# Attention, routing and two expert layers in one launch: smaller pieces of the products, the last 32 tokens gathered as 128 quarter rows, loads moved behind the first gathers

## The chip, the cores and the metric

The kernel is one program on one core of a Trainium2 chip. Its time is the device time of one execution in microseconds (us). TensorE (PE) does the matmuls, VectorE (DVE) and ScalarE (ACT) the elementwise work, GpSimd (POOL) issues the gathers and scatters by index, SyncE (SP) issues the other DMAs. TensorE's granted clock has two levels, 2.4 GHz (1.00 in the profile) and 1.2 GHz (0.50).

## The reference

Three stages follow one another; the second decides which tokens the third computes together.

```python
# 1 attention: B 4, H 8, S 576, D 64, window of 128, linear bias
scores = where(mask, scale * q @ k.T + bias, -1e9)
x = softmax(scores) @ v                     # -> 2304 tokens x 512
# 2 routing and experts: 8 experts of cap = 288 tokens each
order = argsort(-(x @ w_gate).flatten())
for idx in order:                           # best (token, expert) pair first
    if token is free and the expert has room: assign it
out[mask] = relu(x[mask] @ w1[e]) @ w2[e]   # 512 -> 1024 -> 512
# 3 gated layer, 512 -> 1536 -> 512, every token
g = x @ w_gate;  y = (g * sigmoid(g) * (x @ w_val)) @ w_out
```

The greedy assignment is computed as rounds: the expert that fills first is found, with the threshold at which it has 288 tokens; its tokens are fixed, taken out, and the next round begins.

## The kernel before, in words

**Up to about 165 us** comes attention with the gate's logits, and then the first routing round. After it the program has eight stretches of about 75 us, one for each expert of the order found (k = 0 to 7, "expert 0" to "expert 7" here). In a stretch TensorE computes, for the 288 tokens of expert k:

- the transposes of the gathered tokens (`turn`, L1122): the tokens arrive as rows, three gathers by `fetch` (L1099, POOL) of 128, 128 and 32 rows of 512 numbers into `xg`, and are turned into four banks of 128 x 288, which are evicted as two float16 halves X (high part on ACT, L1077, low part on DVE, L1084). For a column block there are three transposes: 128 rows, 128 rows, 32 rows;
- h, 8 products of 4 contraction tiles (`layer`, L1153; each tile takes 3 matmuls of 128 x 288, for high and low parts), evicted to P; then o, 4 products of 8 tiles; then gate and value, 24 products of 4 tiles, against the weights GV; all of these stand under L1153;
- the output (L1289): for each of two blocks of 128 tokens 12 tiles of 3 matmuls of 128 x 512; the last 32 tokens of an expert are collected in `PR` and computed for four experts at once. Rows are scaled on ACT (L1294) and scattered by POOL (L1298).

Expert 0 computes in float32 (L1159, L1285) while the weights of the gated layer are still being read (36 pieces of 512 KB, tile `stg`, L324) and split on DVE and ACT. The expert's own weights come in 8 pieces of 512 KB: for expert 0 straight into WE, later through `stw`, rounded on ACT (L1055) with the rest on DVE (L1059).

**Beside this runs the routing round of the next expert** (`route`), mostly on DVE. It searches the threshold digit by digit. A digit of it is a chain: all logits are compared with the candidates (L802), summed by partition into `cn` (L806), added up over the partitions by one small matmul on TensorE (`add_up`, L810, result `rp`), and turned into the digit by short DVE instructions (L813 to L861), after which the next comparison begins. When the threshold is known, L896 and L897 (TensorE) count what lies before each token, DVE works out positions (L902 to L926) and a one-hot table `oc` (L929), L934 (TensorE, 18 matmuls) makes the list of tokens from it, and L939 to L942 (DVE) write the index table `idx`, from which the three gathers start. Round k + 1 runs during expert k.

**The order of instructions is written out by a planner** (`Plan`). Every step is added with an engine, a cost, a due time, and the steps it depends on. For each engine the planner takes the ready step with the earliest due time that can start soon (`soft` steps give way to others), with its own costs, a hand-over time between engines, and `late`, an extra delay after a step's end before anybody may use it (1.6 for DMAs). The outcome is a fixed list of instructions per engine; at run time an engine runs its list in order and waits where a step isn't ready. A step of products is one item for the planner: it can't put a count's matmul between its matmuls. h is an item of 12 matmuls, o of 24, gate and value of 12, output of 12.

**Banks**: PSUM has a ring of six banks `mm`, given out in the order in which the planner starts their first user.

Of the kernel before, what the change touches and what calls it, by code (L numbers as in the profile page):

```python
# [42 lines left out]
ROUTE = ((12, 58), (-5, 30))  # L43
WA = 7
# [9 lines left out]
HOLD = range(0, 0)  # L54
# [205 lines left out]
def body(ctx, tc, a, out):  # L260
# [55 lines left out]
    def glu_weights(c, due):  # L316
# [41 lines left out]
        add("DMA", dma(2 ** 19), due, fetch, w=[("stg", c)], late=LATE)  # L358
# [17 lines left out]
    with ExitStack() as es:  # L376
# [316 lines left out]
        for c in range(24):  # L693
            glu_weights(c, 2000 + c)
        plan.run(FIT[0], need)

# [34 lines left out]
    def route(k, due0, due1):  # L731
        v, pos = {}, [0]

        def do(engine, us, fn, r=(), w=(), chain=True):
            pos[0] += 1
            add(engine, us, due0 + (due1 - due0) * min(1.0, pos[0] / (95 if k > 1 else 45)), lambda e: fn(),
                r=[*r, *consts] if pos[0] == 1 else r, w=[("route",)] * chain + [*w], soft=k > 0, port=True)
# [218 lines left out]
        if k < E - 1:  # L956
# [5 lines left out]
            for step, bits in enumerate(FINE if fine else ()):  # L962
# [8 lines left out]
                do("DVE", cost, lambda n=n: by_partition(n))  # L971
# [66 lines left out]
    def weights(k, u):  # L1038
        for c in range(8):
# [3 lines left out]
            def fetch(e, c=c, v=v):  # L1043
                if k not in regs:
                    regs[k] = nc.sync.value_load(eid[k][0:1, 0:1], min_val=0, max_val=E - 1)
                if k == 0:
                    v["f"] = WF[:, c]
                    if c > 3:
# [40 lines left out]
    def tokens(k, u):  # L1089
# [3 lines left out]
        def rows_of(c):  # L1093
            return slice(0, 128) if c < 2 else slice(0, 32)

        def fetch(e, c):
            if ("xg", k) not in T:
                T["xg", k] = wk.tile([128, 3, DM], F32, name="xg", bufs=RINGS["xg"])
# [16 lines left out]

        def turn(e, c, kd):
            if ("X", k) not in T:
                T["X", k] = wk.tile([128, 2, 4, CAP], F16, name="X", bufs=RINGS["X"])
            if ("mm", k, "x", kd) not in T:
                T["mm", k, "x", kd] = bank()  # L1120
            r = rows_of(c)
            nc.tensor.transpose(T["mm", k, "x", kd][:, c * 128:min(CAP, c * 128 + 128)],  # L1122
                                T["xg", k][r, c, kd * 128:kd * 128 + 128], ident[r, r])

        pieces = [[(c, kd) for c in range(3)] for kd in range(4)]
        if k == 0:
            pieces = [[(c, kd) for kd in range(4)] for c in range(3)]
        for n, piece in enumerate(pieces):
            add("PE", 0.083 * len(piece), u - ta + 4 + tn * n, lambda e, piece=piece: [turn(e, *x) for x in piece],
                r=[("xg", k, c) for c, _ in piece] + [("ident",)], w=[("mm", (k, "x", kd), c) for c, kd in piece], soft=k > 0)  # L1130
        for kd in range(4 if k == 0 else 0):
            def whole(e, kd=kd):
                dst = T["X", 0].rearrange("p m k c -> p (m k c)").bitcast(F32).rearrange("p (k c) -> p k c", k=4)[:, kd]
                if e == "ACT":
                    nc.scalar.activation(dst, T["mm", 0, "x", kd][:, :CAP], AF.Copy)
                else:
                    nc.vector.tensor_copy(dst, T["mm", 0, "x", kd][:, :CAP])

            add({"ACT": act(CAP, True), "DVE": dve(CAP)}, None, u - ta + 5 + tn * kd, whole,
                r=[("mm", (k, "x", kd))] + [("mm", (k, "x", kd), c) for c in range(3)],  # L1140
                w=[("X", k, kd, "hi"), ("X", k, kd, "lo")])
        for kd in range(4 if k else 0):
            split(u - ta + 5 + tn * kd, (k, "x", kd), lambda kd=kd: T["mm", k, "x", kd], ("X", k, kd),
# [268 lines left out]
```

## Time and profile before

| what | before |
|---|---|
| median of 3 runs | 850.88 us (849.67 to 853.48) |
| profiled execution | 851.98 us, of which the span is 850.2 |
| TensorE busy | 799.9 us (94%) |
| VectorE busy | 612.7 us (72%) |
| ScalarE / GpSimd busy | 344.8 us (41%) / 138.8 us (16%) |
| TensorE waits from 165 us on: count's matmul L810 | 8.1 us, 10 times |
| TensorE waits from 165 us on: transposes L1122 for gathers | 3.6 us, 4 times |

The profile is of one execution. Its span begins with the first and ends with the last instruction; 1.78 us of the execution lie outside it. Engines run in parallel, so busy shares don't add up; with TensorE at 94%, the time is TensorE's work and its waits.

### The profile page before, as it was taken

What the parts mean: (1) busy time and instruction counts of PE and PEld (TensorE: products, weight loads), DVE (VectorE), ACT (ScalarE), POOL (GpSimd) and SP (SyncE); (2) the same over time, 40 slices, a digit from 0 to 9 for tenths busy, and PEclk for the clock granted to TensorE, in tenths of its full rate; (3) what the DMA queues carried; (4) which work ended last, traced back from release to release, by engine and by line L of the source; (5) the groups of instructions that cost most, each with busy time, mean ns of one, the idle gap of its engine ahead of it and who ended that gap; (6) DMA issues with size and microseconds to landing.
All of it is one profiled execution on the core that took longest, in us unless ns stands there. A gap on an engine that the chain in (4) does not pass through costs nothing.

```text
span 850.2 us, 16631 instructions
## 1 busy us (share of the span) xinstructions
PE 799.9 (94%) x6397; PEld 587.1 (69%) x6397; DVE 612.7 (72%) x1763; ACT 344.8 (41%) x775; POOL 138.8 (16%) x195
## 2 busy tenths in 40 slices
PE   7999994499999999999999999999999999999997
PEld 5888884267765777477667865786678677757763
DVE  3788899979999898689877887888579954312320
ACT  5788883245447424312431242135212543211220
POOL 5677653100003001100110011001100210010001
PEclk9999997589999999999999999999999999999999
DMA  8889612566564003400430051024001561000000
GB/s 265 308 302 330 213 57 81 202 234 204 182 199 165 13 1 110 141 2 1 161 91 1 11 194 61 2 75 152 25 1 54 154 221 51 1 25 1 2 1 37
DMA packets 32064, 92.08 MB, mean 108 GB/s; under 512 B 3952, under 2 KB 10480, under 8 KB 31216
## 3 DMA queue, kind: packets, MB, share of 16 engines
q1 hardware_dynamic: 29008, 81.57, 28.9%
q0 software_dynamic: 2976, 9.44, 3.2%
q8 instruction: 50, 0.82, 0.4%
q14 instruction: 30, 0.25, 0.1%
HBM read 81.56 MB, written 9.44 MB: 107 GB/s over the span
## 4 chain that ended last, share of the span: by engine, by line
PE 69%; issue 11%; DVE 11%; ACT 3%; DMA 2%; POOL 2%; SPq 0%; POOLq 0%; DVEq 0%; ACTq 0%
PE mm L1153 41%; PE mm L1289 10%; PE mm L1159 4%; PE s L549 4%; PE mm L1285 2%; PE o L609 2%; PE t L569 2%; PE mm L1122 2%; DVE cmp L802 1%; DVE cn L806 1%; DMA xg<-x_dram,idx 1%; PE rp L934 1%; DVE tl L584 1%; DVE sc L557 1%; POOL xg L1099 1%
## 5 line engine op out<-in xcount | busy, mean ns | idle before, releaser
L1153 PE MATMUL mm<-O,GV 128*128 128x288 f16 x2304 | 287.5, 286 | 0.0
L1153 PEld LDWEIGHTS <-GV 128*128 128x128 f16 x2304 | 221.9, 98 | 55.4
L1153 PEld LDWEIGHTS <-WE 128*128 128x128 f16 x1344 | 129.8, 98 | 34.2 <-issue 1.0
L1289 PE MATMUL mm<-WO,P 128*128 128x512 f16 x504 | 113.5, 383 | 0.0
L1099 POOL DMA_INDIRECT xg<-x_dram,idx x24 | 25.0, 1041 | 407.9 <-issue 241.6
L1236 ACT ACTIVATE P<-z 128x288 f16<-128x288 f32 x84 | 37.0, 441 | 127.1 <-DVE z L1228 127.1
L1289 PEld LDWEIGHTS <-P 128*128 128x128 f16 x504 | 48.7, 99 | 57.2 <-issue 2.2
L1153 PE MATMUL mm<-P,WE 128*128 128x288 f16 x672 | 84.0, 286 | 0.0
L1153 PE MATMUL mm<-X,WE 128*128 128x288 f16 x672 | 83.9, 286 | 0.0
L1059 DVE SCALAR_TENSOR_TENSOR WE<-stw,WE 128x512 f16<-128x512 f32 x112 | 73.8, 685 | 12.8 <-ACT WE L1055 12.8
L1055 ACT ACTIVATE WE<-stw 128x1024 f16<-128x1024 f32 x56 | 58.3, 1052 | 24.4 <-DMA stw<-in_w_dram 24.3
L1228 DVE SCALAR_TENSOR_TENSOR z<-mm,t 128x288 f32<-128x288 f32 x84 | 38.1, 454 | 38.7 <-PE mm L1153 36.1
L806 DVE TENSOR_REDUCE cn<-cmp 128x56 f16<-128x1008 f16 (+2 forms) x55 | 63.8, 1160 | 1.0
L549 PE MATMUL s<-kt,qb 128*128 128x192 f32 (+2 forms) x288 | 58.0, 336 | 5.1 <-DMA kt<-in_kT_dram 5.1
L802 DVE TENSOR_TENSOR cmp<-wm,thr 128x1008 f16<-128x1008 f32 (+1 forms) x50 | 61.0, 1221 | 1.2
L1222 ACT ACTIVATE t<-mm 128x288 f32<-128x288 f32 x96 | 39.1, 407 | 56.0 <-PE mm L1153 54.0
L563 ACT ACTIVATE pb<-sc,mx 128x192 f32<-128x192 f32 (+2 forms) x144 | 56.2, 432 | 10.3 <-DVE mx L557 9.9
L1298 POOL DMA_INDIRECT out_dram<-R,idx x16 | 17.9, 1117 | 239.4 <-ACT R L1294 223.1
L1239 DVE TENSOR_TENSOR P<-z,P 128x288 f16<-128x288 f32 x84 | 38.3, 456 | 20.4 <-ACT P L1236 20.1
L557 DVE CUSTOM_DVE_ANT_0 sc<-s,bias 128x192 f32<-128x192 f32 (+2 forms) x144 | 41.9, 330 | 14.1 <-PE s L549 5.9
L549 PEld LDWEIGHTS s<-kt,qb 128*128 128x128 f32 x288 | 46.7, 203 | 6.8 <-DMA qb<-in_qB_dram 3.9
L1082 DVE SCALAR_TENSOR_TENSOR P<-mm,P 128x288 f16<-128x288 f32 x56 | 25.4, 453 | 28.6 <-ACT P L1077 28.5
(166 smaller groups left out, 1090.8 us busy)
## 6 DMA issues: line engine op xcount, KB each, us to landing
stw<-in_w_dram SPq DMA_DIRECT2D x56, 512.0 KB, 3.9
stg<-in_glu_dram SPq DMA_DIRECT2D x36, 512.0 KB, 4.1
qb<-in_qB_dram SPq DMA_DIRECT2D x3, 2304.0 KB, 10.9
x_dram<-xr SPq DMA_DIRECT2D x16, 256.0 KB, 3.5
WE<-in_w_dram SPq DMA_DIRECT2D x8, 512.0 KB, 5.5
kt<-in_kT_dram SPq DMA_DIRECT2D x3, 1152.0 KB, 7.4
vf<-in_vN_dram SPq DMA_DIRECT2D x8, 256.0 KB, 4.1
vt<-in_vT_dram SPq DMA_DIRECT2D x4, 512.0 KB, 7.9
```

Of the source, the lines that this page charges most:

```text
L549: nc.tensor.matmul(v["s"][:, par, c:], QB[b % 2][:, hp * 9 + i], KT[b % 2][:, hp, (i - 2) * 64 + c:(i + 1) * 64], start=True, stop=True)
L557: nc.vector.tensor_tensor_reduce(out=v["sc"][:, par, c:], in0=v["s"][:, par, c:], in1=bias[:, hp, c:], scale=-0.125, scalar=3.0e38, op0=OP ...
L563: nc.scalar.activation(PB[n % NPB][:, par, 64 * par + c:64 * par + W], v["sc"][:, par, c:], AF.Exp, bias=v["mx"][:, par:par + 1], scale=-1.0)
L802: V.tensor_tensor(v["ca"], v["wm"][:, :, None, :].to_broadcast(by), thr[:, None, :, None].to_broadcast(by), op=OP.is_ge)
L806: V.tensor_reduce(tile_of("cn", [128, E, 8], F16, bufs=1)[:, :, :n], v["ca"], op=OP.add, axis=AX.X)
L1055: nc.scalar.activation(WE[:, c, 0], v["f"], AF.Copy, scale=sc)
L1059: nc.vector.scalar_tensor_tensor(WE[:, c, 1, at], f[:, at], sc, WE[:, c, 0, at], op0=OP.mult, op1=OP.subtract)
L1153: nc.tensor.matmul(p[:, :at.stop - at.start], w(i, k), x[:, j, k, at], start=(m == 0), stop=(m == 3 * nk - 1))
L1222: nc.scalar.activation(v["t"], T["mm", k, ("gv", f, 0)][:, :CAP], AF.Silu, scale=1.0 / (SO * SG))
L1228: nc.vector.scalar_tensor_tensor(v["z"], T["mm", k, ("gv", f, 1)][:, :CAP], SPR / (SO * SG), v["t"], op0=OP.mult, op1=OP.mult)
L1239: nc.vector.tensor_sub(P()[:, 1, f], v["z"], P()[:, 0, f])
L1289: nc.tensor.matmul(T["mm", k, "y", c], x[:, i, kk, at], WO[0][:, kk, j, :], start=(kk == 0 and i == j), stop=(kk == 11 and i == 1))
```

## The change

Four things change.

**Pieces.** Every product is added to the planner in pieces of two contraction tiles (6 matmuls in float16, 2 instructions in float32), and the output too. The arithmetic and its order inside a product stay.

**Count.** `by_partition` has `late=0.6`, so the planner places the count's matmul later on TensorE than it did. The due times of the rounds for experts 2 to 7 are spread over 50 us where they were spread over 35.

**Gather.** The last 32 tokens are fetched as 128 quarter rows: row 4t + q of the view of x with 128 columns goes to partition 32q + i. `listed2` writes that index column with four small DVE instructions in place of one. One 128 x 128 transpose turns them all, where four transposes of 32 rows stood, so a token set has 9 transposes in place of 12, in five banks in place of four: four of 256 columns, one of 128 that holds the 32 last columns of all four blocks. X is evicted in five pairs of instructions.

**Loads.** Before the first gathers, only 11 of the gated layer's 36 weight pieces and 2 of expert 0's 8 pieces may be fetched; the others wait for the three gathers of expert 0 (a small POOL write to their buffer holds them) and come interleaved. Before the change 4 of the 8 could go ahead, and the 36 were held by their ring of three buffers alone.

```diff
-ROUTE = ((12, 58), (-5, 30))
+ROUTE = ((12, 58), (-5, 45))
-HOLD = range(0, 0)
+EARLY_GLU = 11
+HOLD = range(11, 14)
 ...
-        add("DMA", dma(2 ** 19), due, fetch, w=[("stg", c)], late=LATE)
+        add("DMA", dma(2 ** 19), due, fetch, r=[("xg", 0, x) for x in range(3)] if c >= EARLY_GLU else [], w=[("stg", c)], late=LATE)
 ...
             V.tensor_scalar(p2, v["pi"][:, :2], float(N // 2), None, op0=OP.add)
-            V.tensor_scalar(idx[k][:, 2:], v["pi"][:, 2:3], float(N // 2), None, op0=OP.add)
             V.tensor_sub(idx[k][:, :2], p2, v["pi"][:, 1:3])
+            for q in range(4):
+                V.tensor_scalar(idx[k][32 * q:32 * q + 32, 2:], v["pi"][:32, 2:3], 4.0, 2.0 * N + q, op0=OP.mult, op1=OP.add)
 ...
-                do("DVE", cost, lambda n=n: by_partition(n))
+                do("DVE", cost, lambda n=n: by_partition(n), late=0.6)
 ...
-                when = u - WA + (3.9 * c if c < 4 else 15.6 + 3.9 * (c - 4))
-                add("DMA", dma(2 ** 19), when, fetch, r=[("eid", k)] + [("xg", k, x) for x in range(3 if c > 3 else 0)],
+                when = u - WA + 3.9 * c if c < 4 else glu_due(EARLY_GLU + 2 * (c - 4) + 1) + 0.5
+                add("DMA", dma(2 ** 19), when, fetch, r=[("eid", k)] + [("xg", k, x) for x in range(3 if c > 1 else 0)],
 ...
-                out=T["xg", k][rows_of(c), c, :], out_offset=None, in_=x_dram[:, :],
-                in_offset=bass.IndirectOffsetOnAxis(ap=idx[k][rows_of(c), c:c + 1], axis=0))
+                out=T["xg", k][:, part(c)], out_offset=None,
+                in_=x_dram[:, :] if c < 2 else x_dram.rearrange("n (q d) -> (n q) d", q=4),
+                in_offset=bass.IndirectOffsetOnAxis(ap=idx[k][:, c:c + 1], axis=0))
 ...
-        pieces = [[(c, kd) for c in range(3)] for kd in range(4)]
+        pieces = [[(c, kd) for c in range(2)] for kd in range(4)] + [[(2, 4)]]
 ...
-            add("PE", (3 if by is layer else 4) * nk * pe(at.stop - at.start), when, fn, r=r, w=[("mm", (k, name)), ("in order",)])
+            for k0 in range(0, nk, 2):
+                def fn(e, k0=k0):
+                    if k0 == 0:
+                        T["mm", k, name] = bank()
+                    by(T["mm", k, name], w, x(), nk, range(k0, k0 + 2))
+                us = (3 if by is layer else 4) * pe(CAP)
+                add("PE", 2 * us, when + k0 * us, fn, r=r, w=[("mm", (k, name)), ("in order",)])
 ...
-                for kk in range(4 * a, 4 * a + 4):
+                for kk in range(2 * a, 2 * a + 2):
 ...
-            steps = [(a, c) for a in range(3)]
+            steps = [(a, c) for a in range(6)]
```

Three places show what the planner makes of it. Line numbers after the change are 2 to 24 higher. The first is TensorE at the tokens of expert 3, before: the first three of the four groups of transposes, between matmuls of expert 2's output.

```order
5198 L1289 MATMUL mm<-WO,P 128x512
5199 L1122 MATMUL mm<-cst,xg 128x128 x2
5200 L1122 MATMUL mm<-cst,xg 128x32
5201 L1122 MATMUL mm<-cst,xg 128x128 x2
5202 L1122 MATMUL mm<-cst,xg 128x32
5203 L1122 MATMUL mm<-cst,xg 128x128 x2
5204 L1122 MATMUL mm<-cst,xg 128x32
5205 L1289 LDWEIGHTS P
5206 L1289 MATMUL mm<-WO,P 128x512
```

The same place after: the fourth group follows 12 output matmuls later (two transposes), and the single transpose of the last 32 tokens another 12 later.

```order
5177 L1313 MATMUL mm<-WO,P 128x512
5178 L1128 MATMUL mm<-cst,xg 128x128 x6
5179 L1313 LDWEIGHTS P
5180 L1313 MATMUL mm<-WO,P 128x512
5181 L1313 LDWEIGHTS P
```

The nine rows of transposes have become a group of six, and what stands ahead of them is shorter: from L896 to the first transposes TensorE had 48 matmuls of gate and value, L934, then 24 of gate and value and 24 of the output, and now has 42, L934, 24 and 18.

The second is VectorE from the one-hot table to the index table of expert 3, before (`P` and `z` are evictions of the gated layer, `WE` the rest of expert 3's weights).

```order
1063 L929 TENSOR_TENSOR oc<-k_slot,po 128x2304
1064 L1239 TENSOR_TENSOR P<-z,P 128x288
1065 L1059 SCALAR_TENSOR_TENSOR WE<-stw,WE 128x512
1066 L1228 SCALAR_TENSOR_TENSOR z<-mm,t 128x288
1067 L1059 SCALAR_TENSOR_TENSOR WE<-stw,WE 128x512
1068 L1239 TENSOR_TENSOR P<-z,P 128x288
1069 L939 TENSOR_SCALAR p_6317<-rp 128x2
1070 L940 TENSOR_SCALAR idx_2989<-rp 128x1
1071 L941 TENSOR_TENSOR idx_2989<-p_6317,rp 128x2
1072 L942 TENSOR_SCALAR ridx_2994<-rp 32x1
```

And after.

```order
1066 L931 TENSOR_TENSOR oc<-k_slot,po 128x2304
1067 L1263 TENSOR_TENSOR P<-z,P 128x288
1068 L1252 SCALAR_TENSOR_TENSOR z<-mm,t 128x288
1069 L1062 SCALAR_TENSOR_TENSOR WE<-stw,WE 128x512
1070 L1263 TENSOR_TENSOR P<-z,P 128x288
1071 L941 TENSOR_SCALAR p_6323<-rp 128x2
1072 L942 TENSOR_TENSOR idx_2989<-p_6323,rp 128x2
1073 L944 TENSOR_SCALAR idx_2989<-rp 32x1 x4
1074 L945 TENSOR_SCALAR ridx_2994<-rp 32x1
```

One instruction of the weights' rest has moved behind the index table, the column for the last 32 tokens comes after that of the first 256, and it takes four instructions.

The third is SyncE's list of loads around expert 0's weights (WE) and the gated layer's (stg), before.

```order
76 L1052 DMA WE<-in_w_dram 128x1024
77 L1052 ISA
78 L1052 DMA WE<-in_w_dram 128x1024
79 L1052 ISA
80 L1052 DMA WE<-in_w_dram 128x1024
81 L324 DMA stg<-in_glu_dram 128x1024 x2
82 L1052 ISA
83 L1052 DMA WE<-in_w_dram 128x1024
```

And after.

```order
76 L1055 DMA WE<-in_w_dram 128x1024
77 L325 DMA stg<-in_glu_dram 128x1024 x2
78 L1055 ISA
79 L1055 DMA WE<-in_w_dram 128x1024
80 L1055 ISA
81 L1055 DMA WE<-in_w_dram 128x1024
82 L325 DMA stg<-in_glu_dram 128x1024 x2
83 L1055 ISA
84 L1055 DMA WE<-in_w_dram 128x1024
```

Before, four loads of WE stood in a row, then two of stg, then four of WE and 25 of stg; now it is two of WE, two of stg, two of WE, and from there one of WE after every second stg.

## Rows read from the trace of the kernel before

**Rows 1.** The page, part 1: busy time, share of the span, instructions.

```profile
PE 799.9 (94%) x6397; PEld 587.1 (69%) x6397; DVE 612.7 (72%) x1763; ACT 344.8 (41%) x775; POOL 138.8 (16%) x195
```

**Rows 2.** TensorE's waits from 165 us on: total us, times, longest.

```profile
PE rp L810 <- DVE cn L806: 8.1, 10, 1.1
PE mm L1122 <- DMA xg<-x_dram,idx: 3.6, 4, 1.5
...
PE rp L788 <- DVE c L783: 0.4, 1, 0.4
```

**Rows 3.** Timeline of TensorE, transposes: start, duration, line, count; in brackets idle before.

```profile
589.47 0.56 PE L1122 MATMUL mm<-cst,xg 128*128 128x128 f32 x3
589.96 2.76 PE L1289 MATMUL mm<-WO,P 128*128 128x512 f16 x12
...
696.95 2.19 PE L1122 MATMUL mm<-cst,xg 128*128 128x128 f32 x12
```

**Rows 4.** Groups by form, TensorE, 170.3 to 171.1 us: busy, mean ns | idle.

```profile
L1122 PE MATMUL mm<-cst,xg 128*128 128x128 f32 x4 | 0.6, 279 | 1.1 <-issue 1.1
```

**Rows 5.** Timeline of TensorE: runs of product matmuls.

```profile
417.39 5.34 PE L1289 MATMUL mm<-WO,P 128*128 128x512 f16 x24
...
710.84 35.44 PE L1153 MATMUL mm<-O,GV 128*128 128x288 f16 x288
```

**Rows 6.** Timeline of TensorE around the count's matmul L810.

```profile
297.17 3.11 PE L1153 MATMUL mm<-O,GV 128*128 128x288 f16 x24
301.12 0.20 PE L810 MATMUL rp<-cn,k_ones 128*128 128x56 f16 x1 [0.84 <-DVE cn L806]
...
380.83 4.58 PE L1153 MATMUL mm<-O,GV 128*128 128x288 f16 x36
385.24 0.19 PE L810 MATMUL rp<-cn,k_ones 128*128 128x56 f16 x1
```

**Rows 7.** Timeline of VectorE from one count to the next.

```profile
297.38 0.22 DVE L813 TENSOR_REDUCE mo<-rp 128x7 f32<-128x56 f32 x1 [1.96 <-PE rp L810]
...
297.79 0.46 DVE L1084 SCALAR_TENSOR_TENSOR O<-mm,O 128x288 f16<-128x288 f32 x1
...
299.85 1.21 DVE L806 TENSOR_REDUCE cn<-cmp 128x56 f16<-128x1008 f16 x1
```

**Rows 8.** Timeline of TensorE and VectorE, list and tokens of expert 3.

```profile
407.49 6.04 PE L1153 MATMUL mm<-O,GV 128*128 128x288 f16 x48
...
413.37 1.22 PE L934 MATMUL rp<-rh,oc 128*128 128x3 f16 x18
...
416.08 0.15 DVE L939 TENSOR_SCALAR p<-rp 128x2 f32<-128x2 f32 x1
...
422.57 0.27 PE L1122 MATMUL mm<-cst,xg 128*128 128x128 f32 x1
...
423.18 1.59 PE L1122 MATMUL mm<-cst,xg 128*128 128x128 f32 x8 [0.34 <-DMA xg<-x_dram,idx]
```

**Rows 9.** Timeline of TensorE, tokens of expert 2.

```profile
343.35 0.33 PE L1122 MATMUL mm<-cst,xg 128*128 128x128 f32 x1 [0.53 <-DMA xg<-x_dram,idx]
344.90 1.91 PE L1122 MATMUL mm<-cst,xg 32*128 32x32 f32 x10 [1.22 <-DMA xg<-x_dram,idx]
```

**Rows 10.** Windows: length, busy PE, PEld, DVE, ACT, POOL; granted clock, DMA share, GB/s.

```profile
346.60:350.00 3.40, 3.40 (x9) 1.24 (x10) 2.22 (x6) 3.23 (x6) 1.11 (x2) 0.50 0.12 47
421.70:425.10 3.40, 3.06 (x16) 1.59 (x15) 2.62 (x7) 1.11 (x3) 0.00 (x0) 1.00 0.41 127
172.50:179.30 6.80, 6.51 (x26) 4.11 (x26) 3.22 (x7) 0.87 (x3) 0.00 (x0) 0.50 0.94 339
```

**Rows 11.** Timeline of TensorE, tokens of expert 0.

```profile
172.56 1.12 PE L1122 MATMUL mm<-cst,xg 128*128 128x128 f32 x4 [1.54 <-DMA xg<-x_dram,idx]
```

**Rows 12.** Timeline of TensorE between the transposes and the first product of expert 1.

```profile
269.33 3.68 PE L1285 MATMUL mm<-WO,P 128*128 128x512 f32 x8
```

**Rows 13.** All 24 gathers: time from issue to landing.

```profile
DMA to landing us min/median/max: 3.4/4.6/5.4
```

More of the change, by code (lines that the diff above doesn't have):

```diff
@@ L692, in body @@
         need = list(plan.todo)
-        for c in range(24):
+        for c in range(EARLY_GLU):
             glu_weights(c, 2000 + c)
@@ L1120, in turn @@
                 T["mm", k, "x", kd] = bank()
[L1121 to L1125 removed]
+            d0 = part(c).start + (kd * 128 if c < 2 else 0)
+            nc.tensor.transpose(T["mm", k, "x", kd][:, c % 2 * 128:c % 2 * 128 + 128], T["xg", k][:, d0:d0 + 128], ident)
@@ L1126, in tokens @@
+        pieces = [[(c, kd) for c in range(2)] for kd in range(4)] + [[(2, 4)]]
         if k == 0:
-            pieces = [[(c, kd) for kd in range(4)] for c in range(3)]
+            pieces = [[(c, kd) for kd in range(4)] for c in range(2)] + [[(2, 4)]]
         for n, piece in enumerate(pieces):
-            add("PE", 0.083 * len(piece), u - ta + 4 + tn * n, lambda e, piece=piece: [turn(e, *x) for x in piece],
+            add("PE", 0.11 * len(piece), u - ta + 4 + tn * n, lambda e, piece=piece: [turn(e, *x) for x in piece],
@@ L1130, in tokens, with ends @@
                 r=[("xg", k, c) for c, _ in piece] + [("ident",)], w=[("mm", (k, "x", kd), c) for c, kd in piece], soft=k > 0)
-        for kd in range(4 if k == 0 else 0):
-            def whole(e, kd=kd):
-                dst = T["X", 0].rearrange("p m k c -> p (m k c)").bitcast(F32).rearrange("p (k c) -> p k c", k=4)[:, kd]
+        def ends(kd):
+            if kd < 4:
+                return (slice(kd, kd + 1), slice(0, 256)), (lambda: T["mm", k, "x", kd][:, None, :256])
+            return (slice(0, 4), slice(256, CAP)), (lambda: T["mm", k, "x", kd][:, :128].rearrange("p (q i) -> p q i", q=4))
@@ new lines, in tokens, with whole @@
+        for kd in range(5):
+            (ks, cs), src = ends(kd)
+            n = 256 if kd < 4 else 128
+            when, come = u - ta + 5 + tn * kd, [("mm", (k, "x", kd))] + [("mm", (k, "x", kd), c) for c in ((0, 1) if kd < 4 else (2,))]
+            keys = [("X", k, y, n, z) for y in range(4)[ks] for z in ("hi", "lo")]
+            def whole(e, ks=ks, cs=cs, src=src):
+                dst = T["X", 0].rearrange("p m k c -> p (m k c)").bitcast(F32).rearrange("p (k c) -> p k c", k=4)[:, ks, cs]
@@ L1134, in whole @@
                 if e == "ACT":
-                    nc.scalar.activation(dst, T["mm", 0, "x", kd][:, :CAP], AF.Copy)
+                    nc.scalar.activation(dst, src(), AF.Copy)
                 else:
[L1137 to L1141, printed above, removed]
@@ L1146, in body, with layer @@
+            if k == 0:
+                add({"ACT": act(n, True), "DVE": dve(n)}, None, when, whole, r=come, w=keys)
+            else:
+                add("ACT", act(n, True), when, high, r=come, w=keys[::2])
+                add("DVE", dve(n), when, low, r=come + keys[::2], w=keys[1::2])
     T = {}
-    def layer(p, w, x, nk, at=slice(0, CAP)):
-        m = 0
-        for k in range(nk):
+    def layer(p, w, x, nk, ks):
+        for k in ks:
             for i, j in ((0, 0), (1, 0), (0, 1)):
-                nc.tensor.matmul(p[:, :at.stop - at.start], w(i, k), x[:, j, k, at], start=(m == 0), stop=(m == 3 * nk - 1))
-                m += 1
@@ L1156, in layer32 @@
-    def layer32(p, w, x, nk, at=slice(0, CAP)):
-        for k in range(nk):
-            nc.tensor.matmul(p[:, :at.stop - at.start], w(0, k), x[:, k, at], start=(k == 0), stop=(k == nk - 1))
+                nc.tensor.matmul(p[:, :CAP], w(i, k), x[:, j, k, :], start=(k == 0 and i == j), stop=(k == nk - 1 and j == 1))
+    def layer32(p, w, x, nk, ks):
+        for k in ks:
+            nc.tensor.matmul(p[:, :CAP], w(0, k), x[:, k, :], start=(k == 0), stop=(k == nk - 1))
     def both(*key):
@@ L1190, in expert @@
                     [("WE", "hi", f // 2)] + [("WE", "lo", f // 2, x) for x in range(2)]
-                    + [y for kd in range(4) for y in both("X", k, kd)], by=layer32 if first else layer)
+                    + [y for kd in range(4) for n in (256, 128) for y in both("X", k, kd, n)], by=layer32 if first else layer)
             u += 1.95 if first else 1.48
@@ L1338, in split_output_weights @@
             add("DVE", dve(512), when, low, r=[("stg", 100 + kk), ("WO", kk, 0)], w=[("WO", kk, 1)], port=True)
-    for c in range(24, 36):
-        glu_weights(c, glu_due(c))
     for t in plan.todo:
@@ L1348, in body @@
         tokens(k, u)
+        for c in range(EARLY_GLU, 36) if k == 0 else ():
+            glu_weights(c, glu_due(c))
         weights(k, u)
```

33 lines of the change are left out of this document (16 added, 17 removed).

## The prediction

> **What bounds the kernel now.** I read the busy times first: TensorE works 799.9 of 850.2 us [rows 1], so only its work, its clock and its waits can give time back. Second, its waits by line, from 165 us on: ten waits for the sum `cn` before the count's matmul, 8.1 us, and four of the transposes for gathers, 3.6 us, 1.5 of them at expert 0 [rows 2]. Third, the timeline at these places, and windows for the clock. What TensorE does not wait for (ACT, most of VectorE) costs nothing as long as it stays hidden.
>
> **Transposes (A).** In the order before, experts 1 to 7 have 12 each, in groups of three. A group takes 0.49 us from its start to the next output matmul (589.47 to 589.96), and twelve at once take 2.19 [rows 3]. 28 groups at 0.49 to 0.55 are 13.7 to 15.4 us; I take 14.5. How little the 128-wide ones cost shows in four of them in a row: 0.6 us, mean of one 279 ns; so each further one adds (0.6 - 0.28) / 3 = 0.11 [rows 4]. The group of three with its change of operand is 0.49, so the one of 32 rows is the dear one. After the change there are 9 of the cheap sort for each expert, 63 in all: 6.9 us at 0.11, 9.1 at 0.145 (the lower end of what two of the three in a group of 0.49 can leave), and I take 7.6, since they still change operands between groups. A = -6.9 (-5.5 to -8.0).
>
> [...] The rows show that a lone transpose reads about 0.28 us and that neighbours overlap [rows 4]. [...]
>
> **Count waits (B).** At full clock 288 product matmuls take 35.44 us, 0.123 each, and 24 output matmuls 5.34 (0.22) [rows 5]. From one count to the next sum VectorE needs, from L813 at 297.38 to the end of L806 at 301.06, 3.7 us, 0.46 of them an eviction [rows 7]; about 0.2 lie at either end. A gap of 24 product matmuls covers 2.97 and waits 0.84; 36 cover 4.4 and wait for nothing [rows 6]. Eight of the ten waits are such gaps of 24. In the new order nearly all gaps are 36 or 42; 24 stands twice and 30 (3.7 us) about seven times, where 0.1 to 0.4 stays. So 8.1 becomes 2 x 0.85 + 7 x 0.2 = 3.1; B = -4.9. If each 30 also meets a conversion on VectorE that the chain must let by, 6 us stay: -2 to -5.6.
>
> **Gather waits (C).** This is the price. For expert 3, L939 starts at 416.08 and the second transpose at 423.18, when its gather has landed: 7.1 us, and 0.34 of waiting [rows 8]. TensorE's cover from the end of L896 at 407.49 to the first transpose at 422.57 is 15.1: 48 matmuls, L934, 24 and 24. The new order has 42, L934, 24 and 18: 42 x 0.123 + 1.1 + 2.95 + 18 x 0.22 = 13.1, so TensorE arrives 2.0 earlier. VectorE's list comes earlier too: one L1059 (0.6) has moved behind it, one eviction (0.37) has moved ahead of L896, and the later of the two evictions between waits less for ACT; 0.7 to 1.4 in all. The wait grows to 0.34 + 2.0 - (0.7 to 1.4) = 0.9 to 1.6; I take 1.15. The covers of experts 1, 2, 4, 5 and 6 are within 0.5 of that, worked out in the same way; expert 7 has 96 product matmuls between and waits for nothing. Six waits of 1.1 are 6.6 against 2.1 before (0.34 and, at expert 2, 0.53 + 1.22 [rows 8, 9]): C = +4.5 (0 to +7.5). The third gather no longer counts, since 24 or more matmuls come before its transpose. The four small index instructions follow the columns of the first two gathers and delay only the third.
>
> **Clock (D).** After expert 2's transposes, where TensorE had waits of 1.75 and transposes only until 346.8 [rows 9], the granted clock is 0.50 from 346.6 to 350.0; after expert 3's 2.1 us of such it stays at 1.00 [rows 10]. Work of 1.7 us took 3.4. With one wait near 1.1 and six transposes (0.7) the stretch without products is about 1.9 and nearer to expert 3's. Taken: expert 2's fall goes in 7 of 10 cases, D = -1.2; bounds -1.7, and +3.4 if three others fall.
>
> **Expert 0 to 1 (E).** Before, 3.7 us of float32 output matmuls lay between the transposes and the first product of X [rows 12] and hid X's eviction. Now the single transpose and one count are all that stands there; the eviction on ACT and then on VectorE (0.46 for such a one [rows 7]) is in the open: 0.3 of transpose, 0.4 and part of 0.46. E = +1.0 (0.4 to 2). At the other experts 24 output matmuls (5.3 us) hide it.
>
> **Routing for expert 1 (F)** is cut finer by smaller pieces: 0.74 of cover (6 x 0.123) where 1.48 stood, and half as much in float32 too. It waited once, 0.4 [rows 2]; some of the new gaps fall short by tenths: +0.5 (0 to +2.5).
>
> **Loads (G).** TensorE waits 1.54 at 172.56 for the second gather of expert 0 [rows 11]. Two loads of 512 KB fewer stand before it, but all 24 gathers land in 3.4 to 5.4 us [rows 13], expert 3's at a DMA share of 0.41 in rows 10 no faster than the median, so load in front has little hold on them. One transpose in place of four at the end, and X's copies can start earlier: G = -0.4 (-2 to +0.5). The held loads are hidden by expert 0's first products: pieces 4 to 7 of WE belong to the second matrix and are read after all of h, 8 products of 4 tiles in float32, each longer than the 1.48 us of one in float16, so over 12 us; should that cover fail, a late piece costs what is left of its landing, some us, and the range's upper end holds it.
>
> A rule speaks for more here. The rows show landings that hardly depend on the DMA share [rows 13]. "DMA: Bandwidth & Descriptors", Queues, rings and completion order, says that each DMA engine goes round between the queues that have work; fewer loads ahead would then shorten the gathers. By it the whole of the 1.54 could go, and what follows is the third rival below.
>
> **Sum.** -6.9 - 4.9 + 4.5 - 1.2 + 1.0 + 0.5 - 0.4 = -7.4. The profiled execution took 851.98 (span 850.2, and 1.78 outside it); it would take 844.6. That execution lies 1.1 above the median of 850.88, so in the median's terms 843.5.
>
> **Rivals.**
>
> 1. *The gathers become the bound (slower).* Place: the six transitions. If the list gains nothing on VectorE, each transition waits 0.34 + 2.0 = 2.3, 13.8 in all, +11.7 over before; and each then has a stretch without products like expert 2's, with a fall of 1.7: six are 10.2, where before had one, +8.5. With A, B, E, F and G (-10.7) that is +9.5: 860.4. For it: expert 2, where just this happened at 1.75. Against it: L1059 has moved, and expert 3's row. It turns slower than before when a wait passes 0.7 with falls at all six, or 2.4 without any.
> 2. *No gain.* TensorE is only freed to wait: VectorE works most of the time, and a search that gets less cover at one place loses what it gains at another. If the count waits stay at 8.1 (B = 0) and the gather waits reach 1.6 each (C = +7.5) the sum is -6.9 + 7.5 - 1.2 + 1.0 + 0.5 - 0.4 = +0.5: 851. For it: the eight old waits and the new shorter covers are the same kind of place. Against it: the chain's length is measured and 42 matmuls cover it by 1.4.
> 3. *The start gains more.* Without the wait of 1.54 the clock may stay up through 172.5 to 179.3, where it was 0.50 for 6.8 us, 3.4 of them lost [rows 10]; with the sum above, -7.4 - 1.1 - 3.4 = -11.9: 839. Against it: TensorE was busy 6.51 of the 6.80 us of that stretch, so that its clock was not low for want of work there, and the landings of rows 13.
>
> **Numbers.** My forecast has 0.62, rival 1 0.10, rival 2 0.15, rival 3 0.13. Half a per cent, 4.3 us, is what a measurement of this kernel can tell from no change: faster is below 846.6, slower above 855.1. Faster: 0.58 of the forecast's cases and rival 3's, and 0.03 of rival 2: 0.74. Slower: rival 1's upper part, 0.07, and 0.02 of rival 2: 0.09. The rest, 0.17, is the same. The likeliest case's own range is 840 to 848 (A, B and C at their ends partly cancel, since a wait saved at a count arrives at the gather sooner); with the other cases 837.5 to 852.5.
>
> **What would show it.** Right: transposes of experts 1 to 7 take 7 to 9 us in all; L810's waits total 2.5 to 4; L1122's successor waits about 1.1 at six places, on the gather of `xg`; L934 runs straight through; a wait of about a microsecond before the first product of expert 1. Wrong: waits of over 2 at the transitions with a granted clock of 0.50 behind them; count waits still near 8; a wait of products for `WE` or `GV` between 175 and 205, which would mean that the held loads come too late; a new wait of the transposes for a bank.

## The result, and the profile after

| what | before | after |
|---|---|---|
| median | 850.93 us (849.67 to 853.48, 4 runs) | 841.97 us (840.59 to 843.23, 4 runs) |
| ratio of after to before | | 0.9891, 95% interval 0.9862 to 0.9919 |
| profiled execution (span) | 851.98 (850.2) | 841.45 (839.7) |
| count's matmul waits for VectorE, from 165 us on | 8.1 | 3.4 |
| transposes wait for gathers, experts 1 to 7 | 2.1 | 3.3 |
| transposes of experts 1 to 7 without their waits | 15.0 | 7.8 |

The change made the kernel faster by 9.0 us in the median; 843.5 was forecast, in a range of 837.5 to 852.5. The two profiled executions differ by 10.5. Four of the runs below had one execution far off the others (1038 to 4574 us), and medians and ratios are over the others.

The page of the changed kernel, part 1, and TensorE's waits from 165 us on (total, times, longest):

```profile
PE 791.2 (94%) x6373; PEld 583.5 (69%) x6373; DVE 614.5 (73%) x1795; ACT 345.2 (41%) x782; POOL 139.4 (17%) x200
```

```profile
PE mm L1128 <- DMA xg<-x_dram,idx: 6.1, 6, 2.1
PE rp L812 <- DVE cn L808: 3.4, 7, 0.8
...
PE mm L1174 <- DVE O L1088: 0.5, 1, 0.5
...
PE mm L1174 <- ACT X L1157: 0.3, 1, 0.3
```

Beside [rows 1, 2]: TensorE's work is 8.7 us less, and the order of the two waits is reversed. Of the 6.1 us for gathers 2.8 fall on expert 0, at 171 and 173 us; the other 3.3 are 2.07 at expert 1, 0.44 at expert 3, and 0.37 and 0.39 at expert 4. The longest one of expert 0 and that of expert 1:

```profile
171.10 0.66 PE L1128 MATMUL mm<-cst,xg 128*128 128x128 f32 x4 [1.93 <-DMA xg<-x_dram,idx]
...
262.37 0.98 PE L1128 MATMUL mm<-cst,xg 128*128 128x128 f32 x7 [2.07 <-DMA xg<-x_dram,idx]
```

The timeline of TensorE at three sets of transposes of the changed kernel (start, duration, what, count):

```profile
339.24 0.60 PE L1128 MATMUL mm<-cst,xg 128*128 128x128 f32 x4
339.67 1.46 PE L1313 MATMUL mm<-WO,P 128*128 128x512 f16 x6
...
579.78 0.38 PE L1128 MATMUL mm<-cst,xg 128*128 128x128 f32 x2
580.00 0.90 PE L1174 MATMUL mm<-O,GV 128*128 128x288 f16 x6
...
687.42 1.15 PE L1128 MATMUL mm<-cst,xg 128*128 128x128 f32 x9
```

Four take 0.43 us up to the next matmul, two take 0.22: 0.11 each, where three with one of 32 rows took 0.49 [rows 3]. The nine in a row end in 1.15 where twelve took 2.19.

The counts of expert 2, in the same view:

```profile
365.73 2.37 PE L1174 MATMUL mm<-P,WE 128*128 128x288 f16 x18
368.44 0.20 PE L812 MATMUL rp<-cn,k_ones 128*128 128x56 f16 x1 [0.34 <-DVE cn L808]
368.48 5.31 PE L1174 MATMUL mm<-P,WE 128*128 128x288 f16 x42
373.63 0.19 PE L812 MATMUL rp<-cn,k_ones 128*128 128x56 f16 x1
```

The gap ahead of the first is 30 matmuls (12 of h, then these 18 of o) and waits 0.34; these 42 wait for nothing. These answer to [rows 6]. But not every longer gap is covered. Here is the count ahead of them, behind 48 matmuls (6 of the output, 42 of h), with what VectorE did at the start of that gap:

```profile
352.93 1.29 DVE L1062 SCALAR_TENSOR_TENSOR WE<-stw,WE 128x512 f16<-128x512 f32 x2 [1.83 <-ACT WE L1058]
354.14 0.18 DVE L815 TENSOR_REDUCE mo<-rp 128x3 f32<-128x24 f32 x1
...
359.06 0.19 PE L812 MATMUL rp<-cn,k_ones 128*128 128x56 f16 x1 [0.56 <-DVE cn L808]
```

The digit's first instruction, L815, stands in VectorE's order behind two instructions for the rest of the expert's weights, which waited for ACT.

The list and the tokens of expert 3, TensorE and VectorE, answer to [rows 8]:

```profile
405.98 5.30 PE L1174 MATMUL mm<-O,GV 128*128 128x288 f16 x42
411.12 1.22 PE L936 MATMUL rp<-rh,oc 128*128 128x3 f16 x18
...
413.23 0.15 DVE L941 TENSOR_SCALAR p<-rp 128x2 f32<-128x2 f32 x1
...
419.23 0.33 PE L1128 MATMUL mm<-cst,xg 128*128 128x128 f32 x1
420.00 0.77 PE L1128 MATMUL mm<-cst,xg 128*128 128x128 f32 x5 [0.44 <-DMA xg<-x_dram,idx]
```

From the end of L898 (405.98) to the first transpose are 13.2 us, from L941 to the second 6.8.

And two windows (length, busy PE, PEld, DVE, ACT, POOL; granted clock, DMA share, GB/s), expert 2's transposes and expert 0's first products:

```profile
339.20:346.90 7.70, 7.70 (x41) 4.10 (x40) 5.83 (x13) 2.98 (x7) 0.54 (x1) 1.00 0.16 58
173.50:180.30 6.80, 6.75 (x16) 4.20 (x17) 3.44 (x11) 1.50 (x4) 0.40 (x3) 0.50 0.57 175
```

Expert 2's tokens cost no wait and no fall of the clock. At expert 0 the low stretch is as long as before [rows 10], 6.8 us, but begins with the first product (173.56) where it began 2.4 us ahead of it.

### The profile page after: what moved, and what is told of

The parts are those of the page before. It is cut to its first block, busy times and chain, and to the rows that moved or that the text cites. A ratio compares the mean times of both kernels' runs of the same rounds, so it can differ in the third digit from the quotient of the medians.

```text
span 839.7 us, 16655 instructions
## 1 busy us (share of the span) xinstructions
PE 791.2 (94%) x6373; PEld 583.5 (69%) x6373; DVE 614.5 (73%) x1795; ACT 345.2 (41%) x782; POOL 139.4 (17%) x200
## 4 chain that ended last, share of the span: by engine, by line
PE 55%; issue 10%; DVE 7%; DMA 4%; ACT 1%; POOL 1%; POOLq 0%; SPq 0%; DVEq 0%; ACTq 0%
PE mm L1174 39%; PE mm L1313 9%; PE mm L1179 4%; DMA xg<-x_dram,idx 2%; DMA stw<-in_w_dram 2%; DVE cn L808 1%; DVE cmp L804 1%; PE mm L1309 1%; PE mm L1128 1%; DVE P L1086 1%; PE rp L936 1%; DVE WE L1062 1%; ACT WE L1058 0%; PE rp L812 0%; POOL out_dram L1322 0%
## 5 line engine op out<-in xcount | busy, mean ns | idle before, releaser
L558 DVE CUSTOM_DVE_ANT_0 sc<-s,bias 128x192 f32<-128x192 f32 (+2 forms) x144 | 41.8, 329 | 13.5 <-PE s L550 11.8
```

The costliest lines, as they stand in the source:

```text
L558: nc.vector.tensor_tensor_reduce(out=v["sc"][:, par, c:], in0=v["s"][:, par, c:], in1=bias[:, hp, c:], scale=-0.125, scalar=3.0e38, op0=OP ...
```

## The experiments

All twelve were timed in five rounds against the kernel before on the same chip. "Parts" are the four of the change: gather, pieces, delay (the `late` of the count, 0.6), loads; and the spread of the rounds' due times (35 us before, 50 after). The changed kernel has all, at 0.9891. Of an edit the lines that say what it does are shown; " ..." marks what is left out.

| run | parts | median us | ratio to before (95%) |
|---|---|---|---|
| no_gather | all but gather | 845.81 | 0.9942 (0.9923 to 0.9960) |
| no_late | all but delay | 842.07 | 0.9896 (0.9879 to 0.9913) |
| no_pieces | all but pieces | 857.12 | 1.0070 (1.0045 to 1.0094) |
| no_loads | all but loads | 840.73 | 0.9880 (0.9860 to 0.9900) |
| no_route | all, spread 35 | 840.64 | 0.9891 (0.9868 to 0.9914) |
| only_gather | gather | 847.94 | 0.9968 (0.9956 to 0.9980) |
| only_pieces | pieces | 848.78 | 0.9985 (0.9971 to 0.9998) |
| only_route | spread 50 | 853.11 | 1.0021 (1.0007 to 1.0035) |
| gp_route | gather, pieces, spread 50 | 843.15 | 0.9914 (0.9899 to 0.9928) |
| best | gather, pieces, delay, spread 43 | 845.37 | 0.9927 (0.9914 to 0.9940) |
| route60 | gather, pieces, delay, spread 65 | 837.75 | 0.9853 (0.9839 to 0.9867) |
| after60 | all, spread 65 | 836.03 | 0.9821 (0.9803 to 0.9840) |

**One part undone.** First the gather:

```diff
 ...
-        pieces = [[(c, kd) for c in range(2)] for kd in range(4)] + [[(2, 4)]]
+        pieces = [[(c, kd) for c in range(3)] for kd in range(4)]
 ...
```

> The changed kernel with the old gather of the last 32 tokens: 12 transposes for each expert, four of them of 32 rows, X evicted in four pieces of 288 columns; pieces, late count and moved loads stay. Theory (the 12 against 9 transposes were worth 7.2 us, as the two traces show: 15.0 against 7.8 in experts 1 to 7 without waits): the transposes' time comes back to 15 us, and since these groups stand later after the list (9.2 us of cover against 7.9) the gathers are waited for less, by about 1: near 848 (846 to 850). Rival (the gain of the transposes only freed TensorE to wait, the count's place is what paid): 842 to 844.

Measured 845.8: 3.8 above the changed kernel, between the two. In its trace, of the slowest of its executions (849.45), the transposes do take 15.1 us again, and the gathers after expert 0 wait 2.6 in place of 3.3. What the transposes do to the time is told by only_gather below.

The count's delay:

```diff
 ...
-                do("DVE", cost, lambda n=n: by_partition(n), late=0.6)
+                do("DVE", cost, lambda n=n: by_partition(n))
```

> The changed kernel without the extra delay of 0.6 on by_partition; all else stays. In its order nine gaps between counts hold 24 product matmuls (3.0 us) and one holds 30, where the changed kernel has two and seven. Theory (a chain of 3.7 to 3.9 us waits about 0.85 behind each cover of 3.0): count waits of 8 to 9 against 3.4, and longer covers of the gathers (10 us at experts 3 and 4) that save 0.8: 846 (844.5 to 847.5). Rival (the smaller pieces alone took the count's waits away): within 1 us of 842.

842.07, the rival's number, but not for its reason. TensorE's waits in its profile:

```profile
PE rp L812 <- DVE cn L808: 8.8, 11, 0.8
PE mm L1128 <- DMA xg<-x_dram,idx: 3.2, 2, 2.3
```

The counts wait as long as in the kernel before; the gathers wait 0.96 in all after expert 0, where the changed kernel has 3.3. So 5.4 us more at one place came with 2.3 less at the other. Of the 3.1 left, 0.7 came back before o of expert 0 (its first product at 192.64 against 193.36) and 0.5 at the transposes; the two profiled executions differ by 0.8, and the rest I can't place. In these two kernels taking the count's waits away is worth nothing that the medians show.

The pieces:

```diff
 ...
-            for k0 in range(0, nk, 2):
+            for k0 in range(0, nk, nk):
 ...
-            steps = [(a, c) for a in range(6)]
+            steps = [(a, c) for a in range(3)]
 ...
```

> The changed kernel with products and output in the old pieces (whole products of 12 or 24 matmuls, output in 12); new gather, late count and moved loads stay. Its order has no gap under 3.9 us between counts, but only 6.3 us from the list to the transposes at experts 2 and 3. Theory (waits are read off the covers): count waits near 0 (-3.4 against the changed kernel), gather waits of 1.5 to 2.2 each at those two with a fall of the clock of 1.7 behind one or both (+5 to +8 against its 0.4): 844 to 847. Rival (small pieces are what the gain rests on, by themselves): 849 or more. Second rival (the pieces are worth nothing): 841 to 843.

857.12: the size of the gather's waits was missed. Its waits:

```profile
PE mm L1128 <- DMA xg<-x_dram,idx: 18.1, 14, 2.6
PE mm L1175 <- ACT X L1157: 1.6, 4, 0.4
```

There is no count wait at all. But the delay pushes each digit behind a whole product (48 matmuls between counts where 42 stood), the list comes later, and the transposes stand 6.3 us behind it with no output matmuls among them. A shorter cover is not all of it: the second gathers of experts 2 and 3 landed 6.3 and 5.7 us after their issue, where they took 3.9 in the changed kernel, and the median of all 24 was 5.5 against 4.0. So about half of these waits is slower landing, and why the gathers were slower here no run shows. Expert 3's, and the windows behind the tokens of experts 2 and 3:

```profile
434.10 0.33 PE L1128 MATMUL mm<-cst,xg 128*128 128x128 f32 x1 [2.57 <-DMA xg<-x_dram,idx]
435.44 1.97 PE L1128 MATMUL mm<-cst,xg 128*128 128x128 f32 x8 [1.01 <-DMA xg<-x_dram,idx]
437.84 0.40 PE L1175 MATMUL mm<-X,WE 128*128 128x288 f16 x1 [0.43 <-ACT X L1157]
```

```profile
353.30:356.60 3.30, 2.87 (x13) 1.52 (x12) 3.23 (x9) 1.99 (x6) 0.00 (x0) 0.50 0.03 14
435.20:442.00 6.80, 6.13 (x27) 4.23 (x28) 4.41 (x12) 3.67 (x8) 0.00 (x0) 0.50 0.36 102
```

This is the slower rival of the prediction, waits of over 2 with the clock at 0.50 behind them, in a kernel that lacks one of the four parts. Ahead of the second fall TensorE had only a wait and transposes, from 431.5 on.

The loads:

```diff
-EARLY_GLU = 11
-HOLD = range(11, 14)
+HOLD = range(0, 0)
 ...
```

> The changed kernel with the loads of the kernel before (four WE loads before the first gathers, the weight pieces not held). Theory (the loads moved to 200 to 241 us and expert 1's weights behind them make its gather land 6.5 us after issue, which is the wait of 2.07 us at 262 us, and what the start gains is about 1.3 to the first product, half of it lost to the clock again): within 1.5 us of the changed kernel's 842, with a shorter wait at expert 1 and the first product of expert 0 about 1 us later. Rival (the held loads are what shortened the start by 0.85 us before the list and 0.5 behind it, and stay won): 843.5 to 845, the first product at 174.9 as before.

840.73, as the theory had it, and the first product at 174.16 against 173.56, 0.6 later where it said about 1. Expert 1's second gather issues at 254.96, and its transposes run at 259.30 without a wait. The window 258 to 262 us of this kernel, and then the same of the changed one:

```profile
258.00:262.00 4.00, 4.00 (x17) 2.27 (x16) 3.90 (x12) 1.85 (x5) 0.00 (x0) 1.00 0.86 252
```

```profile
258.00:262.00 4.00, 2.30 (x7) 0.78 (x5) 3.27 (x9) 0.00 (x0) 0.32 (x2) 1.00 0.94 339
```

What was saved went at the next step: the first product of expert 1 waited 1.82 for X's last eviction (0.34 in the changed kernel), and the clock fell once behind it (0.51 granted over 273.4 to 276.8 us).

**One part alone.**

```diff
-            V.tensor_scalar(idx[k][:, 2:], v["pi"][:, 2:3], float(N // 2), None, op0=OP.add)
             V.tensor_sub(idx[k][:, :2], p2, v["pi"][:, 1:3])
+            for q in range(4):
+                V.tensor_scalar(idx[k][32 * q:32 * q + 32, 2:], v["pi"][:32, 2:3], 4.0, 2.0 * N + q, op0=OP.mult, op1=OP.add)
 ...
```

> The kernel before with the new gather of the last 32 tokens alone (9 transposes, five evictions); old pieces, old count place, old loads. Its order has the eight gaps of 24 matmuls between counts, as before, and 8.1 to 11.4 us from the list to the transposes. Theory (the transposes are worth 7.2 us wherever they stand): transposes of experts 1 to 7 at about 7.8 us, count waits still 8, gather waits 2 to 3: 843.5 (842 to 845). Rival (undoing this part cost the changed kernel only 3.8, so it is worth about 4, the rest being lost to longer waits for gathers): 846 to 847.5.

847.94: the rival. Its waits:

```profile
PE rp L810 <- DVE cn L806: 8.0, 10, 1.1
PE mm L1125 <- DMA xg<-x_dram,idx: 7.7, 7, 2.0
```

The transposes fall from 15.0 to 8.2 us here too, but the gathers of experts 1 to 7 wait 5.1 in place of 2.1. With the fall behind expert 2 gone (1.7) and 0.6 more at one count of round 1 that is -6.9 + 3.0 - 1.7 + 0.6 = -5.0, and the profiled executions differ by 5.1. (Its profiled execution is the fastest of its eight; the medians differ by 3.3.) So time saved on a step that waits for nothing arrives, in part, as a wait at the next that does.

The pieces alone (both edits of no_pieces, the other way round, on the kernel before):

> The kernel before with the small pieces alone; old gather, old count place, old loads. Its order still has nine gaps of 24 matmuls between counts, but 9.6 to 14.4 us from the list to the transposes. Theory (pieces do not touch the counts' waits without the delay, and pay by starting the gathers earlier under more cover): count waits 8 to 9 as before, gather waits from 2.1 to near 0 and the fall of the clock behind expert 2's (1.7) gone: 847.5 (846 to 849). Rival (pieces are worth what they take off the counts' waits, and that needs the delay): no change, 850 to 851. Second rival (the 16 us by which large pieces made the changed kernel slower are theirs wherever they stand): under 844.

848.78, at the slow end of the theory's range; by the ratio the gain is 1.3 us, between theory and rival. Count waits 9.4, gather waits after expert 0 0.6 and no fall, as it said; it had not priced a count of 1.39 in round 2.

The spread alone:

```diff
-ROUTE = ((12, 58), (-5, 30))
+ROUTE = ((12, 58), (-5, 45))
```

> The kernel before with the rounds' due times spread over 50 us and nothing else. Its order has the same eight gaps of 24 between counts and the same covers but for expert 5 (8.5 us in place of 11.4). Theory (the spread alone moves nothing that matters, since with whole products there are few places to choose from): 850.5 to 851.5, one gather wait more. Rival (the spread pays by itself): 847 or less.

853.11, a gain by no reading: 1.8 us slower by the ratio, which neither theory nor rival had.

**Parts together.** Gather, pieces and spread 50:

> New gather, small pieces and the spread of 50 us, without the count's delay and with the loads of the kernel before: what is left when the two parts that undoing showed to be worth nothing (delay) or less than nothing (held loads, +1.2) are both left out. Theory (the delay trades waits at the count for waits at the gathers one for one, and the loads cost 1 at expert 1's gather): count waits of 8 to 9, no gather wait from expert 2 on: 841 (839.5 to 842.5). Rival (the delay is needed once the gathers of expert 1 are no longer late): 844 to 846.

843.15, between theory and rival. By their ratios, gather, pieces and spread alone make -2.7, -1.3 and +1.8 us, -2.2 together; in one kernel they make -7.3. What is different is the gather: after expert 0 it waits 0.2 in all in this kernel and 5.1 in only_gather. At experts 3 and 4 TensorE has 10 us between list and transposes where it had 9.2 and 8.1. But more of it is that the tokens come sooner: from the end of the list's matmuls to the landing of the second gather are 5.9, 6.9 and 6.7 us at experts 1 to 3, where only_gather has 8.8, 9.1 and 9.4. At expert 1 the cover is the same in both, and the gather itself took 3.5 us in place of 6.5.

**The planner's numbers.** Spread 35 in the changed kernel (`(-5, 30)`):

> The changed kernel with the due times of the rounds for experts 2 to 7 spread over 35 us as before, in place of 50; all else stays. Its order has three gaps of 24 matmuls between counts and six of 30, covers of 7.9 to 8.1 us at experts 2 to 4 and 11.4 at expert 5. Theory (waits are read off the covers, which hardly differ): count waits 4, gather waits at most 1 beside that of expert 1: 842 (840.5 to 843.5). Rival (the spread is worth several us by itself, as 43 in place of 50 cost 4.6 without the moved loads): 845 to 847.

840.64, as the theory said. Spread 43 without the loads (`(-5, 38)`):

> The changed kernel with the loads of the kernel before and the rounds' due times spread over 43 us in place of 50. Its order has one gap of 24 between counts where the changed kernel has two and no_loads three, with covers of the gathers of 7.7 to 8.1 us. Theory (waits are read off the covers): count waits 2.5 to 3, gather waits at experts 2 to 6 up to 1, the rest as no_loads: 840 (838.5 to 841.5). Rival (each wait saved at a count is given back at the next gather): 841 to 842, as no_loads and the changed kernel.

845.37: wrong by 5. The counts waited 6.4 in twelve places. I had held each gap against one length of chain, but at expert 4 even 24 output matmuls, 5.3 us, did not cover one. VectorE ahead of that chain, and TensorE's wait at its end:

```profile
513.81 1.29 DVE L1060 SCALAR_TENSOR_TENSOR WE<-stw,WE 128x512 f16<-128x512 f32 x2 [2.52 <-ACT WE L1056]
515.02 0.17 DVE L813 TENSOR_REDUCE mo<-rp 128x3 f32<-128x24 f32 x1
```

```profile
518.76 0.19 PE L810 MATMUL rp<-cn,k_ones 128*128 128x56 f16 x1 [0.93 <-DVE cn L806]
```

The count's matmul had run at 512.46. VectorE has two instructions for the rest of the expert's weights ahead of L813 in its order. They waited 2.52 us for ACT, whose own rounding had waited 2.76 for a load of weights (`stw`); the digit began 2.4 us late. So a cover is worth what stands in the order of the other engine too. The same happened at 355 us, and in the changed kernel at 353 (the rows of 359.06 above).

Spread 65 without the loads (`(-5, 60)`):

> New gather, small pieces and the count's delay, loads as before the change, and the rounds' due times spread over 65 us in place of 50. Its order has no gap of 24 between counts and four of 30, and 8.3 us of cover from the list to the transposes at experts 3 to 5 (7.9 with 50). Theory (waits are read off the covers): count waits of about 1 against 3.3, gather waits under 1 from expert 2 on: 838.5 (837 to 840). Rival (what is saved at counts comes back as later lists and gather waits): 841 to 843. Second rival (any step of the planner's numbers moves the time by 3 to 5 us in either direction, as the step to 43 did): 844 or more.

837.75, as said, and below the changed kernel. Its waits:

```profile
PE mm L1125 <- DMA xg<-x_dram,idx: 4.3, 5, 1.5
PE mm L1171 <- ACT X L1154: 1.4, 1, 1.4
...
PE rp L810 <- DVE cn L806: 0.5, 1, 0.5
```

And the changed kernel with that spread, one number of it edited:

```diff
-ROUTE = ((12, 58), (-5, 45))
+ROUTE = ((12, 58), (-5, 60))
```

> The changed kernel, held loads included, with the rounds' due times spread over 65 us in place of 50: one number. It is route60 with the held loads. Theory (loads still in flight at 258 to 262 us make the second gather of expert 1 land over 5 us after its issue, as in the four kernels run with new gather and held loads, where it cost 1.0 to 2.1; without held loads and with small pieces no kernel waited there): a wait of 1 to 2 at expert 1's second gather, the first product of expert 1 waiting 0.3 in place of 1.4 on ACT, so that 0 to 1 of it stays, and 838 to 839.5 in all against route60's 837.75. Rival (the wait there comes of how early the list is, not of the loads): no wait of over 0.5 at expert 1, 836.5 to 838.

836.03, the fastest of all: the rival's time, with the theory's wait. It does wait 1.32 at expert 1's second gather (issued at 259.56, in at 265.4), so five of five kernels with new gather and held loads wait there, 1.0 to 2.1, and four of four with new gather, small pieces and the old loads don't. So in these kernels the held loads do make that gather late: 6.5 us in the changed kernel, 3.5 in no_loads. They aren't needed for it, since in only_gather (old loads, large pieces) it took 6.5 us too and TensorE waited 1.80. That the held loads cost time in the end is not shown: 840.73 against 841.97 and 837.75 against 836.03 point opposite ways.

## Why the prediction was right

The time came out 1.5 us under the forecast, and that closeness is in part luck: between the two profiled executions, for which the sum was made, the gain is 10.5 where 7.4 was forecast, and the errors of the terms partly cancel. What was right is the mechanism: transposes and counts give about 12 us back, and a part of it is paid at the gathers. The terms, forecast and then by the two traces:

| term | forecast | traces |
|---|---|---|
| A, transposes | -6.9 | -7.2 (15.0 to 7.8) |
| B, count waits | -4.9 | -4.7 (8.1 to 3.4) |
| C, gather waits | +4.5 | +1.2 (2.1 to 3.3) |
| D, clock behind expert 2 | -1.2 | -1.7, no new fall |
| E, expert 0 to 1 | +1.0 | +0.3 (a wait of 0.34; the transpose is in A) |
| F, routing for expert 1 | +0.5 | -0.2 (0.4 to 0.2 at its waits) |
| G, loads | -0.4 | -0.3 |
| not forecast: gate and value of expert 1 wait for O, at 301 us | 0 | +0.5 |
| sum | -7.4 | -12.1, against -10.5 measured in the two executions |

- **A** holds as priced: the pitch of 0.11, the time that each further transpose adds, is seen directly at groups of two and four. "TensorE: Matmul & The Clock Gate", Part 4: PE-mode transpose, of the Trainium skill gives about 275 ns for a 128x128 one inside a kernel (bf16 there, float32 here). Taken as the price of each, that would be an estimate of 5.8 for the 84 less 63; the trace agrees with it as the length of a single one (median 273 ns), and the nine in 1.15 us decide for the pitch.
- **B** has the right size, in part by luck (its own sum, 8.1 less 3.1, is 5.0 and not 4.9). By the chain's length, four gaps of 30 waited 0.3 each and the one gap of 24 waited 0.80: 2.1 us. The other 1.3 are two waits behind 42 and 48 matmuls (0.78 and 0.56), where VectorE's order has weights ahead of the chain or between its steps; the prediction had no term for that, though two of the ten waits of before stood behind 36 and 48 matmuls. That the waits went because of the delay the runs show: with the delay and large pieces (no_pieces) no count waits, and with small pieces and no delay (no_late, only_pieces, gp_route) they total 8.6 to 9.4. The delay alone, on the kernel before, was not run.
- **C** is the term that was mis-sized. Six waits of 1.1 were forecast and there were three, of 2.07, 0.44 and 0.76. At expert 3, for which 1.15 was worked out, cover fell by 1.83 (15.08 to 13.25), but the list came earlier by 1.34 counted from L896's end (8.59 to 7.25), the upper end of the 0.7 to 1.4, and the gather was in 0.33 sooner after L939 (7.10 to 6.77): 0.34 + 1.83 - 1.34 - 0.33 = 0.5, found 0.44. Landing was taken as fixed by the one row of before; its median over all gathers went from 4.6 [rows 13] to 4.0. Experts 2, 5 and 6 show best what the term left out: from the end of the list's matmuls to the landing of the second gather they took 8.4, 8.2 and 8.2 us before and 6.4, 6.2 and 6.9 after, so that a cover of 6.9, 6.5 and 6.9 was enough. Expert 1's was forecast at 1.1 like the others and is the one for which rows of before had no wait to read.
- **G**: the first product came 1.3 us earlier, 0.85 of it ahead of the list, but the second gather waited 1.93 in place of 1.54, and of the 1.3 only 0.3 is left at the end of h, since the low clock now lies wholly on products. The 0.85 can't be put down to the loads: over all fourteen traces the first gather was issued at 163.8 to 166.2 us with the old loads and at 164.0 to 166.0 with the held ones. "Little hold" of the loads on landing rested on a misread row besides: the share of 0.41 in [rows 10] is that of 421.7 to 425.1 us, when expert 3's second gather, issued at 418.49, was nearly in; over its first 4 us the share was 0.84. The third rival, a start that gains 4.5 more, did not come: neither the wait nor the low stretch went.
- **The slower rival** came true in its waits and falls, if not by its cause (a list that gains nothing on VectorE), in no_pieces and not in the changed kernel. There waits of 2.3 to 3.6 at four transitions have a fall each, and the three with 1.0 to 1.8 have none. Against the changed kernel's profile these waits are 12.5 us more and the falls cost about 10, the counts give 3.4 back, and the two executions differ by 18.3. Its points of no gain (a wait of 2.4 at each transition without falls, 0.7 with) no run tests.
- **No gain**, the second rival, is what only_gather and no_late show in part: a little under half of a saving went to the next wait.

1.6 us of the terms' sum aren't found in the time. 0.9 of it lies at the 74 places from 190 us on where a product stands right before a small matmul of the routing: from the start of the one to the start of the other, without the waits listed above, are 12.6 us in all before and 13.5 after, so the finer order also has waits too short for the list. For the other 0.7 no run tells where they went.

Of the signs named ahead, the transposes (7.8 us) and the counts (3.4) came as said; waits of about 1.1 at six places and one of about a microsecond before the first product of expert 1 (it was 0.34) did not.

## What to carry to other kernels

A saving on a busy engine is worth its whole size only if the work it waits for next is early enough; so count the cover from the last input to the wait in both orders before adding up gains. Parts of a change that are planned together can't be priced one at a time: here three parts made 2.2 us apart and 7.3 together, and one left out of four turned 1.1% of gain into 0.7% of loss. Count also what stands ahead of a chain in the other engine's order, not only the matmuls that cover it. After such a change the planner's own numbers are worth a scan (65 us of spread was 6 us faster than 50); whether 65 would have helped the kernel before too was not run.

## What was not expected of the hardware

A gather's time to landing varies more than the prediction allowed: 3.4 to 5.4 us in the kernel before [rows 13], and 2.8 to 8.3 over all fourteen traces. The longest is the third gather of expert 0 in after60, 128 rows of 512 bytes, issued at 166.88 us. Here is TensorE's wait for it; the clock was 0.50 from 170.9 to 184.5, and this execution took 840.17 against the median of 836.03.

```profile
175.33 0.45 PE L1128 MATMUL mm<-cst,xg 128*128 128x128 f32 x1 [3.58 <-DMA xg<-x_dram,idx]
```

How long the clock stays at 0.50 around that place varies too: 6.8 us in nine of the fourteen traces, 10.2 in four, 13.7 in this one.

What else is loading does not explain the landings by itself. The rule weighed in the prediction, from "DMA: Bandwidth & Descriptors", Queues, rings and completion order, of the Trainium skill (a DMA engine goes round between the queues that have work), fits a part of what expert 1's second gather did: it landed 5.4 to 6.5 us after issue with 339 to 355 GB/s moved from 258 to 262 us (after, no_late, no_route), and 3.4 to 3.6 with 219 to 252 (no_loads, gp_route, route60). But it landed in 4.7 under 352 GB/s in the kernel before and in 4.1 under 344 in no_gather, both with the old gather, and took 6.5 under 297 in only_gather. So "little hold" was wrong for some of these kernels, and what makes the gather late in them stays open.
